# Fused chunked attention and MoE layer on one core: attention values as one 64-column product per head instead of two 32-column products

## The chip, the cores and the metric

The kernel runs on one core of a Trainium2 chip. The metric is the device time of one execution in microseconds (us). Three runs of the kernel before gave 625.8, 627.71 and 628.86 us; the median is 627.71 us.

## What is computed

Two stages, one after the other. First attention in chunks: batch 4, 8 heads, 768 positions, head width 64. Each chunk of 32 queries of a head sees its own 32 keys, 16 to the left, 8 to the right, and 8 memory keys, 64 keys in all. Cut to what matters:

```python
for c in range(nc):                                    # 24 chunks of 32 queries
    k_full = np.concatenate([mem_k, k_ctx], axis=2)    # 8 memory + 56 context rows
    v_full = np.concatenate([mem_v, v_ctx], axis=2)
    scores = scale * np.matmul(q_c, k_full.transpose(0, 1, 3, 2))
    a = softmax(scores)
    out[:, :, c_start:c_end] = np.matmul(a, v_full)    # the values: 32 queries x 64 columns
...
x = attn_out as (3072 tokens, 512)
h = x @ w_in                                           # 512 -> 2048
g = s * relu(h)**2 + b
return g @ w_out                                       # 2048 -> 512
```

## The kernel before, in words

**Tiling.** The 3072 tokens are worked on in 8 chunks of 384 (a "chunk" from here on; the 32-query pieces are called cells). For each chunk there are 16 steps, one per 128 columns of the hidden layer. A step has a first product (`hidden`, line 610: 12 matmuls of 128 loaded columns and 384 moved columns), four ScalarE passes and one VectorE pass (lines 618 to 622), and a second product (`result`, line 633: 9 matmuls of 512 moved columns, two steps later). Operands are split into a high and a low part, which is why there are three matmuls where one product is meant. So one step is 21 matmuls with 21 weight loads on TensorE, 42 instructions.

**Attention** for a later chunk is worked out between the steps of the chunks before it. One call of `attend` takes four heads (two pairs, `p`) of one chunk. From the third chunk on (`alone` is false) it lays one fixed row of TensorE work, called a block here: the values of the attention call before (`value1`, `value2`, one per pair, line 502), then the scores of this call (`scores1`, `scores2`, line 481). Lines 561 to 571 chain these four, so that nothing stands between them. Most blocks are eight steps apart; the first two are six apart. There are 12 value parts in the kernel, the first at 145 us; the last one has no scores behind it.

**The value product** (`value`, lines 490 to 503). The loaded operand is the value tile `vals_[p]`: 128 rows are two cells of 64 keys, and 64 columns are one head's width. The moved operand is the block-diagonal tile `aT`: 64 columns, 32 queries for each of the two cells. Output rows are the 64 columns of the head, head `n` on rows 64n to 64n+63. Before, each head's 64 columns are loaded in two parts of 32, each into a quarter of the array's columns:

```python
for n, e in ((n, e) for n in range(2) for e in range(0, D, CHUNK)) if not alone else ():
    nc.tensor.matmul(V[p].tile[n * D + e:n * D + e + CHUNK, to:to + 2 * CHUNK], vals_[p].tile[:, at(n) + e:at(n) + e + CHUNK],
                     aT[n].tile[:, 2 * p + m, c, :], start=True, stop=True)
```

These operands are plain fp32, and each such matmul is carried out as two pairs of a load and a matmul. So a pair of heads is 2 x 3 x 4 = 24 products, 48 loads and 48 matmuls; both pairs are 96 and 96. The scores of a block are likewise 96 and 96. A block is 384 instructions.

For the first two chunks (`alone`) another form stands in line 498: 64 loaded columns and 32 moved ones, in quarters of 64 rows by 64 columns. The change does not touch it.

**Order.** The order of instructions on every engine is made ahead by a planner (`Plan.lay`). It simulates the engines with a cost for each kind of operation (`HOLD`, line 80, in ns), starts whatever is ready with the lowest due time, and the program is written out in that order. The costs steer the order alone; nothing waits for them on the chip. There are no loops or branches left in the program: every instruction stands in it once.

## Time and profile before

| what | value |
|---|---|
| median of three runs | 627.71 us |
| the profiled execution's own time | 625.31 us |
| its span, first to last instruction | 623.5 us |
| granted TensorE clock, mean | 0.996 |
| TensorE matmul (PE) busy | 97% of the span |
| weight load (PEld) busy | 85% |
| VectorE, ScalarE busy | 55%, 55% |
| chain that ended last | PE 82%, DVE 11%, DMA 4%, issue 2%, ACT 1% |

How to read it. Times are microseconds unless marked ns. PE is TensorE's matmul, PEld its weight load, which runs beside the matmuls. "128*32" behind an instruction is the part of the array that it uses, rows by columns; "128x64" is the moved operand of a matmul, or the loaded operand of a load. A row of the timeline gives the start, the length up to the end of the last instruction in it, the instruction, how many of them follow one another, and in brackets the idle time before it and what ended it. "issue" is time in which the engine waited for nothing that the profile shows. Ends of matmuls are modelled, so distances between starts are the safer measure. A row of stretches gives the stretch, its length, and for each engine the busy time and the number of instructions.

### The profile page before, as it was taken

What the parts mean: (1) busy time and instruction counts of PE and PEld (TensorE: products, weight loads), DVE (VectorE), ACT (ScalarE), POOL (GpSimd) and SP (SyncE); (2) the same over time, 40 slices, a digit from 0 to 9 for tenths busy, and PEclk for the clock granted to TensorE, in tenths of its full rate; (3) what the DMA queues carried; (4) which work ended last, traced back from release to release, by engine and by line L of the source; (5) the groups of instructions that cost most, each with busy time, mean ns of one, the idle gap of its engine ahead of it and who ended that gap; (6) DMA issues with size and microseconds to landing.
All of it is one profiled execution on the core that took longest, in us unless ns stands there. A gap on an engine that the chain in (4) does not pass through costs nothing.

```text
span 623.5 us, 13759 instructions
## 1 busy us (share of the span) xinstructions
PE 605.3 (97%) x5854; PEld 532.3 (85%) x5861; DVE 341.3 (55%) x816; ACT 343.7 (55%) x660; POOL 37.2 (6%) x46
## 2 busy tenths in 40 slices
PE   8898999999999999999999999999999999999997
PEld 5667888888989898898988899898988989899996
DVE  6899999884565462825538182654618355131112
ACT  3577888854555554454455555545555445545543
POOL 2112000000010000101001010100101000000000
PEclk9899999999999999999999999999999999999999
DMA  9944766413041300303022030312103110010001
GB/s 348 400 159 145 243 188 183 131 50 129 1 128 50 112 18 12 134 34 128 1 82 98 2 128 1 129 50 77 53 2 127 52 53 0 2 50 2 1 0 52
DMA packets 17342, 55.42 MB, mean 89 GB/s; under 512 B 1920, under 2 KB 1920, under 8 KB 17280
## 3 DMA queue, kind: packets, MB, share of 16 engines
q1 hardware_dynamic: 17280, 54.53, 25.4%
q8 instruction: 46, 0.75, 0.5%
q14 instruction: 16, 0.13, 0.1%
HBM read 48.24 MB, written 6.29 MB: 87 GB/s over the span
## 4 chain that ended last, share of the span: by engine, by line
PE 82%; DVE 11%; DMA 4%; issue 2%; ACT 1%; POOL 0%; DVEq 0%; SPq 0%; ACTq 0%
PE ps L610 37%; PE ps L633 37%; DMA words<-w 4%; PE ps L502 3%; PE ps L481 3%; DVE wv L591 2%; DVE wv L593 2%; PE ps L371 1%; DVE top L419 1%; DVE t L420 1%; DVE den L422 1%; DVE gL L622 1%; DVE w L597 1%; DVE ww L597 1%; DVE words L589 1%
## 5 line engine op out<-in xcount | busy, mean ns | idle before, releaser
L622 DVE TENSOR_TENSOR gL<-ps,gH 128x384 fp32r<-128x384 f32 x128 | 70.9, 555 | 232.1 <-ACT gH L621 231.2
L618 ACT ACTIVATE ps<-ps 128x384 f32<-128x384 f32 x128 | 60.8, 475 | 191.5 <-PE ps L610 190.5
L610 PE MATMUL ps<-xH,w 128*128 128x384 f32 x512 | 130.9, 336 | 0.3 <-DVE w L597 0.3
L610 PE MATMUL ps<-xH,ww 128*128 128x384 f32 x512 | 130.7, 336 | 0.0
L633 PE MATMUL ps<-w,gH 128*128 128x512 f32 x384 | 119.1, 391 | 0.0
L633 PE MATMUL ps<-ww,gH 128*128 128x512 f32 x384 | 119.0, 391 | 0.0
L610 PEld LDWEIGHTS ps<-xH,w 128*128 128x128 f32 x512 | 92.7, 188 | 3.0 <-DVE w L597 0.9
L610 PEld LDWEIGHTS ps<-xH,ww 128*128 128x128 f32 x512 | 92.8, 188 | 2.2
L440 DVE STREAM_TRANSPOSE aT<-t 32x128 f32<-32x128 f32 x288 | 86.9, 302 | 7.2 <-POOL t L425 2.7
L610 PE MATMUL ps<-xL,w 128*128 128x384 f32 x256 | 87.4, 341 | 2.0 <-DVE top L419 1.3
L610 PE MATMUL ps<-xL,ww 128*128 128x384 f32 x256 | 86.8, 339 | 0.0
L620 ACT ACTIVATE ps<-ps,b_sb,s_sb 128x384 f32<-128x384 f32 x128 | 82.3, 643 | 4.2
L633 PEld LDWEIGHTS ps<-ww,gH 128*128 128x128 f32 x384 | 72.1, 188 | 13.3
L633 PEld LDWEIGHTS ps<-w,gH 128*128 128x128 f32 x384 | 72.1, 188 | 13.2
L633 PE MATMUL ps<-w,gL 128*128 128x512 f32 x192 | 76.3, 398 | 1.2 <-DVE gL L622 1.0
L633 PE MATMUL ps<-ww,gL 128*128 128x512 f32 x192 | 75.9, 395 | 1.1 <-DVE gL L622 1.1
L621 ACT ACTIVATE gH<-ps 128x384 fp32r<-128x384 f32 x128 | 62.9, 491 | 3.9
L619 ACT ACTIVATE ps<-ps 128x384 f32<-128x384 f32 x128 | 60.8, 475 | 4.0
L425 POOL TENSOR_TENSOR t<-t,rden 96x512 f32<-96x512 f32 (+1 forms) x36 | 34.8, 967 | 471.2 <-DVE rden L424 372.9
L610 PEld LDWEIGHTS ps<-xL,w 128*128 128x128 f32 x256 | 48.0, 187 | 5.4 <-DVE top L419 1.4
L610 PEld LDWEIGHTS ps<-xL,ww 128*128 128x128 f32 x256 | 48.0, 187 | 2.8
L633 PEld LDWEIGHTS ps<-w,gL 128*128 128x128 f32 x192 | 36.0, 187 | 8.7 <-DVE gL L622 2.4
(51 smaller groups left out, 439.9 us busy)
## 6 DMA issues: line engine op xcount, KB each, us to landing
raw<-qkv SPq DMA_DIRECT2D x28, 576.0 KB, 6.0
words<-w SPq DMA_DIRECT2D x24, 512.0 KB, 4.0
v<-qkv SPq DMA_DIRECT2D x28, 384.0 KB, 3.9
out<-partial SPq DMA_DIRECT2D x24, 256.0 KB, 2.1
early<-w SPq DMA_DIRECT2D x8, 512.0 KB, 10.5
early<-qkv SPq DMA_DIRECT2D x3, 576.0 KB, 6.4
early<-qkv SPq DMA_DIRECT2D x4, 384.0 KB, 8.5
early<-qkv SPq DMA_DIRECT2D x1, 577.0 KB, 3.7
```

What stands on the lines that cost most here:

```text
L425: op("POOL", "norm" + size, late + 0.25, lambda: nc.gpsimd.tensor_tensor(tv(), tv(), wide(rden), ALU.mult), (st["r", key],), (t[key],), lo ...
L440: nc.vector.transpose(aT.tile[rows, :, c, r * CHUNK:(r + 1) * CHUNK], t.tile[c * CHUNK:(c + 1) * CHUNK, r::2, g * CHUNK:(g + 1) * CHUNK])
L481: nc.tensor.matmul(S[n].tile[c * CHUNK:(c + 1) * CHUNK, (at * GB + j) * CELL:(at * GB + j + 1) * CELL], raw.tile[rows, k * CHUNK:(k + 1) * ...
L502: nc.tensor.matmul(V[p].tile[n * D + e:n * D + e + CHUNK, to:to + 2 * CHUNK], vals_[p].tile[:, at(n) + e:at(n) + e + CHUNK], aT[n].tile[:, ...
L591: op("DVE", "wjoin", due, lambda: nc.vector.scalar_tensor_tensor(bits(), bits(), 3, lo(), ALU.logical_shift_left, ALU.bitwise_or), (raw["l ...
L610: nc.tensor.matmul(h.tile[:, :TOK], weight_tile(0, f)[:, wi, c * P:(c + 1) * P], xt(x, xi, c), start=(c == 0 and n == 0), stop=(c == NC_T ...
L618: op("ACT", "relu", u, lambda: nc.scalar.activation(hp(), hp(), AF.Relu), (), (h[0],))
L619: op("ACT", "square", u, lambda: nc.scalar.activation(hp(), hp(), AF.Square), (), (h[0],))
L620: op("ACT", "affine", u, lambda: nc.scalar.activation(hp(), hp(), AF.Identity, scale=s_sb, bias=b_sb), (c_s[0], c_b[0]), (h[0],))
L621: op("ACT", "high", u, lambda: nc.scalar.activation(g.tile[0], hp(), AF.Copy), (h[0],), (g["H"],))
L622: op("DVE", "low", u, lambda: nc.vector.tensor_tensor(g.tile[1], hp(), g.tile[0].bitcast(F32), ALU.subtract), (h[0], g["H"]), (g["L"],))
L633: nc.tensor.matmul(acc.tile, g.tile[gi][:, t * P:(t + 1) * P], weight_tile(1, f)[:, wi, :], start=(first and n == 0), stop=(last and n == 2))
```

## The change

The cost of `value1` and `value2` in the planner's table goes from 670 to 730 ns, and the value product from the third chunk on takes a head's 64 columns at once:

```diff
-HOLD = dict(hidden=523, result=690, scores=560, value1=670, value2=670, scores1=540, scores2=540, turn=84, value=1300, wrest=1000, warm=215,
+HOLD = dict(hidden=523, result=690, scores=560, value1=730, value2=730, scores1=540, scores2=540, turn=84, value=1300, wrest=1000, warm=215,
...
-                    for n, e in ((n, e) for n in range(2) for e in range(0, D, CHUNK)) if not alone else ():
+                    for n in range(2) if not alone else ():
                         to = (m * NQC + c) * 2 * CHUNK
-                        nc.tensor.matmul(V[p].tile[n * D + e:n * D + e + CHUNK, to:to + 2 * CHUNK], vals_[p].tile[:, at(n) + e:at(n) + e + CHUNK],
+                        nc.tensor.matmul(V[p].tile[n * D:(n + 1) * D, to:to + 2 * CHUNK], vals_[p].tile[:, at(n):at(n) + D],
                                          aT[n].tile[:, 2 * p + m, c, :], start=True, stop=True)
```

The same numbers are multiplied and the same output rows are written. A product uses half of the array's columns instead of a quarter, and there are half as many products: 12 for a pair of heads instead of 24.

## Rows read from the trace of the kernel before

**Rows 1.** The page, busy time, share of the span and instructions of each engine.
```profile
PE 605.3 (97%) x5854; PEld 532.3 (85%) x5861; DVE 341.3 (55%) x816; ACT 343.7 (55%) x660; POOL 37.2 (6%) x46
```

**Rows 2.** Waits of PE, 145 to 620 us: total us, times, longest us.
```profile
PE ps L481 <- issue: 4.5, 4, 1.2
PE ps L610 <- DVE top L419: 1.3, 1, 1.3
```

**Rows 3.** Timeline of PE, the block at 284 us.
```profile
284.11 1.55 PE L502 MATMUL ps<-aT,v 128*32 128x64 f32 x96
285.59 1.04 PE L481 MATMUL ps<-raw 64*32 64x64 f32 x80
287.84 0.41 PE L481 MATMUL ps<-raw 64*32 64x64 f32 x16 [1.21 <-issue]
288.18 0.45 PE L610 MATMUL ps<-xL,w 128*128 128x384 f32 x1
```

**Rows 4.** Timeline of PE, the block at 358 us.
```profile
357.98 1.55 PE L502 MATMUL ps<-aT,v 128*32 128x64 f32 x96
...
360.61 0.44 PE L610 MATMUL ps<-xL,w 128*128 128x384 f32 x1
```

**Rows 5.** Timeline of PE, four more blocks: 145, 247, 466 and 504 us.
```profile
145.30 1.55 PE L502 MATMUL ps<-aT,v 128*32 128x64 f32 x96
146.78 0.95 PE L481 MATMUL ps<-raw 64*32 64x64 f32 x70
...
149.29 0.44 PE L610 MATMUL ps<-xL,ww 128*128 128x384 f32 x1
...
246.65 1.55 PE L502 MATMUL ps<-aT,v 128*32 128x64 f32 x96
...
250.62 0.45 PE L610 MATMUL ps<-xL,ww 128*128 128x384 f32 x1
...
466.21 1.55 PE L502 MATMUL ps<-aT,v 128*32 128x64 f32 x96
...
470.08 0.44 PE L610 MATMUL ps<-xL,ww 128*128 128x384 f32 x1
...
503.53 1.55 PE L502 MATMUL ps<-aT,v 128*32 128x64 f32 x96
...
507.49 0.44 PE L610 MATMUL ps<-xL,w 128*128 128x384 f32 x1 [1.28 <-DVE top L419]
```

**Rows 6.** Stretches from the end of one long gap to the end of the next.
```profile
148.80:250.00 101.20, 100.09 (x1024) 90.34 (x1024) 53.55 (x139) 52.25 (x100) 6.24 (x6) 1.00 0.20 67
250.00:287.82 37.82, 36.59 (x384) 32.96 (x384) 19.42 (x49) 18.81 (x36) 2.08 (x2) 1.00 0.22 75
287.82:469.70 181.88, 180.82 (x1792) 163.05 (x1792) 91.71 (x236) 94.05 (x180) 10.41 (x10) 1.00 0.18 64
469.70:507.48 37.78, 36.50 (x384) 32.82 (x384) 20.56 (x52) 18.81 (x36) 2.08 (x2) 1.00 0.23 80
```

**Rows 7.** DMA queues, instruction kind: whole run; 285.4 to 286.5 us; 428.7 to 429.9 us.
```profile
q8 instruction: 46, 0.75, 0.5%
...
q8 instruction: 1, 0.02, 5.2%
...
q8 instruction: 1, 0.02, 4.9%
```

**Rows 8.** Stretches from the end of a long gap to the start of a block.
```profile
148.80:430.12 281.32, 278.96 (x2672) 251.51 (x2672) 145.36 (x375) 145.09 (x278) 16.65 (x16) 1.00 0.20 67
...
469.70:503.52 33.82, 33.81 (x192) 30.40 (x192) 17.74 (x46) 17.59 (x34) 2.08 (x2) 1.00 0.20 71
```

**Rows 9.** Loads of 32 and 64 columns (busy us, mean ns, idle), and PE's timeline at 45 us.
```profile
L502 PEld LDWEIGHTS ps<-aT,v 128*32 128x32 f32 x1152 | 16.6, 110 | 4.1 <-issue 4.1
...
L498 PEld LDWEIGHTS ps<-aT,v 64*64 64x64 f32 x192 | 3.0, 135 | 0.6 <-issue 0.6
...
45.00 1.60 PE L498 MATMUL ps<-aT,v 64*64 64x32 f32 x96
```

## The prediction

> **What bounds the kernel now.** The page first: TensorE's matmuls fill 97% of the span, VectorE and ScalarE 55% each [rows 1]. So time can come only from TensorE: from the length of its work or from its idle time. The list of waits then says where it is idle behind 145 us, where the changed code runs: four times in the scores, with nothing that the profile can name as the cause ("issue"), and once at the first matmul of a step, 5.8 us in all [rows 2]. No wait for another engine is left in the value parts. The last one is put down to a VectorE instruction which that matmul does not read from; I take it for one of the same kind, for a reason that follows.

> The timeline shows what such a gap is. A clean block runs from 357.98 to 360.61, 2.63 us [rows 4]. The block at 284 us stops 80 matmuls into its scores and takes 4.07 us [rows 3]. The four others with a gap take 3.99, 3.97, 3.87 and 3.96 us [rows 5]. Over the clean length they lose 1.44 + 1.36 + 1.34 + 1.24 + 1.33 = **6.7 us**. The other six blocks with scores have no gap; the one at 358 us stands for them.

> Why in five blocks and not in all? Count where the border of a piece falls. At 504 us, 384 instructions lie between the end of a gap and the block's start [rows 8], so a border is 128 instructions into the block and the next at 384, its end: a gap. At 284 us the gap comes after 192 + 160 = 352 instructions [rows 3], so the border before it is at 96. At 145 us it comes after 332 [rows 5]: 76. The same count gives 48 and 80 for the blocks at 247 and 466 us. At 430 us, 5344 instructions after a border [rows 8], borders fall at 32 and 288, and there is no gap: the fetch packet is already seen at 428.7 to 429.9 us, before the block, since TensorE reads ahead over the slow steps. In the block at 284 us the border at 96 is passed at about 284.11 + 96 x 1.48/192 = 284.85, the packet lies within 285.4 to 286.5 [rows 7], and work goes on at 287.84. So the next piece is usable 3.0 us after its border is passed (the same sum gives 2.9 at 145 and 3.0 at 504 us). A block burns 256 instructions in under 2 us. A gap needs **two borders in one block**, the first of them not read ahead: 48 to 128 here.

> **The change, part by part.**

> *Half the instructions.* A value part goes from 96 loads and 96 matmuls to 48 and 48; a block from 384 instructions to 288. Two borders fit inside only when the first is within the first 32 instructions, and up to there they were read ahead (the block at 430 us). A period of eight steps is 8 x 42 + 384 = 720 instructions before and 624 after. So the first borders of the twelve value parts, before at 76, 208, 0, 48, 96, 144, 192, 240, 32, 80, 128, 152, will be at 76, 48, 192, 80, 224, 112, 0, 144, 32, 176, 64, 184. The tightest is 48: passed about 0.75 us into the block, the next border 16 instructions behind the block's end. A step's instruction takes 33.82/384 = 0.088 us [rows 8], so it is reached 2.7 + 1.4 = 4.1 us into the block, 3.3 us after the first; 3.0 are needed. A small margin, and a miss would cost some tenths. I take all five gaps as gone: **-6.7 us**. Nothing else holds these places: the clean blocks show no wait for another engine behind them, so what is late next is again TensorE's own work.

> *The value product's own pace.* Per pair of heads and pass, a group of four quarter-array products becomes a group of two half-array ones; there are 24 groups in a part before and after, and each still moves 64 columns. What is new is that 64 columns are loaded in the time of such a move. The trace has no load of 64 columns beside 64 moved ones. Nearest is line 498: 64 loaded, 32 moved, also 24 groups, 1.60 us [rows 9] against 1.55 [rows 3], so +0.05 us a part, +0.6 us for 12. The planner's own cost in the diff says 60 ns more for each of 24 products, 1.44 us; its old 670 ns fits what the trace shows (two are 1.34 of the 1.48 us from the value part's start to the scores' [rows 3]). Between 0.6 and 1.4 I take **+1.0 us**. Downward: if instructions alone set the pace, half of them at the scores' 1.15/192 = 6.0 ns would save 0.9 us a part, 11 us in all. I leave it out: the value part now takes 7.7 ns an instruction, more than the scores do on the same engine, so issue is not its limit, and the 24 moves stay. Upward: loads not covered by moves. 32 more columns cost a load 135 - 110 = 25 ns [rows 9], so one of 64 is some 50 ns; wholly in the open that is 50 ns x 24 x 12 = 14.4 us, and if only the added 25 ns shows, 7.2 us.

> *The planner's new cost.* It moves the planned end of a block by 0.12 us and so may swap instructions behind 145 us; before the first value part nothing moves. I price it at nothing: what covers it is VectorE's and ScalarE's 45% of idle time and the absence of waits on them in [rows 2]. If a swap made TensorE wait, one wait would be of the size of the 1.3 us there.

> *What stays.* The change of array form at each end of the value part, the semaphores, the loads of `raw` and `v`, the reads of the result by ScalarE. The value tiles come free within 0.1 us of before, and no queue is passed.

> **Sum.** -6.7 + 1.0 = -5.7 us. Against the profiled execution's 625.31 us that is 619.6 us. That execution lies 2.4 us under the median of the three runs shown; on the median, 627.71 - 5.7 = **622.0 us**.

> **The rivals.** About 0.5%, 3.1 us, is what a measurement of this kernel can tell from no change.

> *Loads in the open (other side).* Two half-array products leave less to run beside a load than four quarter ones. The place is the group of [rows 3], the price 0 to 50 ns a group, 288 groups. At 23 ns it eats the 6.7 us, at 34 ns the kernel is slower by over 0.5%; wholly in the open it is 627.71 - 6.7 + 14.4 = 635.4 us. For it: no such group is in the trace. Against it: loads are busy 85% and matmuls 97% of the same span [rows 1], and line 498's longer loads cost it only 2 ns a group. With only the added 25 ns showing it is 628.2, no change. I give 0.08 to slower and 0.06 to this middle. [...]

> *The gaps are not fetches, or stay.* If the count by 256 is a coincidence or TensorE's next piece is late for another reason, the 6.7 us stay and the pace adds 1.0: 628.7 us, no change. For it: the profile names no cause. Against it: four counts that are all exact multiples of 256. Chance 0.05. [...]

> *Gaps move.* The border rule is read from eleven blocks; if the reading ahead starts a little later than I think, blocks with borders at 32, 48 or 64 keep one. Two gaps of 1.3 us left make it 624.6; chance 0.07, half of it within 0.5%. A swap by the planner that costs two such waits comes to the same; 0.03 more.

> **How the numbers follow.** My case, 622.0 us, has 0.71. Faster by over 0.5%: 0.71 + 0.05 (moved gaps or swaps) = 0.76. Within 0.5%: 0.06 + 0.05 + 0.05 = 0.16. Slower: 0.08. The range starts at 619.0, the lowest run before (625.8) less 6.7 and rounded down, with no pace lost, and ends at 625.5, which takes in two gaps that stay, and a pace 12 ns a group worse than I take it; beyond it lie 0.2.

> **What would show it.** No gap over 0.5 us in any of the eleven blocks, each about 2.7 us from first value matmul to first matmul of a step; 576 value matmuls and 576 loads in place of 1152 each; about 41 instruction packets in place of 46 (1152 fewer instructions are 4.5 pieces); the value part at 1.50 to 1.60 us from its start to the scores'. The prediction is wrong if a gap of over 1 us stands in a block with one border only, or if the value part takes over 2 us.

## The result, and the profile after

The changed kernel takes 619.39 us (median of 4 runs, 618.72 to 619.74), the kernel before 627.89 us (4 runs, 625.8 to 628.86). The ratio is 0.9865, 95% interval 0.9846 to 0.9884: 8.5 us faster, where 5.7 us were forecast. The profiled execution took 619.60 us, with a span of 617.8 us.

The page of the kernel after, the same line as [rows 1]:

```profile
PE 605.0 (98%) x5278; PEld 533.3 (86%) x5285; DVE 341.2 (55%) x816; ACT 344.1 (56%) x660; POOL 37.2 (6%) x46
```

There are 576 matmuls and 576 loads fewer, and TensorE's busy time is the same to 0.3 us: what went is idle time. The view of waits that gave [rows 2] lists nothing at all for PE now between 140 and 612 us. The order of the work on all engines is the one of before, instruction by instruction but for the value products; so the planner's new cost moved nothing.

The timeline of two blocks of the kernel after, the fifth (which had a gap before, [rows 3]) and the seventh (which had none, [rows 4]):

```profile
281.92 1.62 PE L502 MATMUL ps<-aT,v 128*64 128x64 f32 x48
283.47 1.22 PE L481 MATMUL ps<-raw 64*32 64x64 f32 x96
284.62 0.45 PE L610 MATMUL ps<-xL,w 128*128 128x384 f32 x1
...
354.48 1.62 PE L502 MATMUL ps<-aT,v 128*64 128x64 f32 x48
...
357.18 0.45 PE L610 MATMUL ps<-xL,w 128*128 128x384 f32 x1
```

Both take 2.70 us from the first value matmul to the first matmul of the step. Before, they took 4.07 and 2.63. The scores run through without a stop (96 in one row). The value part is 283.47 - 281.92 = 1.55 us long instead of 1.48. All eleven blocks with scores are alike to 0.03 us.

The loads by form, to be read beside [rows 9], and the instruction queue, beside [rows 7]:

```profile
L502 PEld LDWEIGHTS ps<-aT,v 128*64 128x64 f32 x576 | 17.8, 138 | 4.1 <-issue 4.1
```

```profile
q8 instruction: 41, 0.67, 0.5%
```

A load of 64 columns is 28 ns longer than one of 32 (138 against 110), there are half as many, and TensorE's program came in 41 packets instead of 46.

### The profile page after: what moved, and what is told of

Read it like the earlier page. It is cut to its first block, busy times and chain, and to the rows that moved or that the text cites. A ratio compares the mean times of both kernels' runs of the same rounds, so it can differ in the third digit from the quotient of the medians.

```text
span 617.8 us, 12607 instructions
## 1 busy us (share of the span) xinstructions
PE 605.0 (98%) x5278; PEld 533.3 (86%) x5285; DVE 341.2 (55%) x816; ACT 344.1 (56%) x660; POOL 37.2 (6%) x46
## 4 chain that ended last, share of the span: by engine, by line
PE 82%; DVE 11%; DMA 3%; ACT 2%; issue 1%; POOL 0%; DVEq 0%; SPq 0%; ACTq 0%
PE ps L610 37%; PE ps L633 37%; DMA words<-w 3%; PE ps L502 3%; PE ps L481 2%; DVE wv L591 2%; DVE wv L593 2%; PE ps L371 1%; DVE t L420 1%; DVE top L419 1%; DVE ww L597 1%; DVE gL L622 1%; DVE den L422 1%; DVE w L597 1%; DVE words L589 1%
```

## The experiments

Two questions were open: whether the gaps really stand where borders between pieces of 256 instructions fall, and why the gain was 8.5 us and not 5.7. Every kernel was compared with the kernel before on the same chip.

### The program shifted by 112 and by 64 instructions

The kernel before, with small matmuls into an unused bank ahead of everything (56 of them, or 32); nothing else differs.

```diff
     with tc.manual_schedule():
+        for _ in range(56):
+            nc.tensor.matmul(idle[:, :64], ones[:, :P], ones[:, :64], start=True, stop=True)
         for _, _, fn in laid:
             fn()
```

> The kernel before with 56 small matmuls (112 instructions) put ahead of everything, so that every border of a piece falls 112 instructions earlier in the program's own work. Theory: first borders in the eleven blocks move from 76, 208, 0, 48, 96, 144, 192, 240, 32, 80, 128 to 220, 96, 144, 192, 240, 32, 80, 128, 176, 224, 16; so there are three gaps, in the 2nd, 7th and 8th block (near 174, 358 and 394 us), none of the five places of before, and about 2.7 us less idle time behind 145 us. The added matmuls may cost 0 to 3 us at the start. Rival (gaps belong to these places of the work, or to the data): the same five blocks have them.

> The same with 32 small matmuls (64 instructions). Theory: first borders at 12, 144, 192, 240, 32, 80, 128, 176, 224, 16, 64; three gaps, in the 6th, 7th and 11th block (near 322, 358 and 504 us); the one in the 11th block was there before, 2.7 us less idle time behind 145 us. Rival: the same five blocks as before.

Ratios 0.9972 (0.9954 to 0.9990) and 0.9982 (0.9971 to 0.9994). PE's timeline of the kernel shifted by 112, the 2nd, 7th and 8th block, and the 4th, which had a gap before:

```profile
174.13 1.55 PE L502 MATMUL ps<-aT,v 128*32 128x64 f32 x96
175.60 1.04 PE L481 MATMUL ps<-raw 64*32 64x64 f32 x80
177.92 0.41 PE L481 MATMUL ps<-raw 64*32 64x64 f32 x16 [1.27 <-issue]
...
356.39 1.55 PE L502 MATMUL ps<-aT,v 128*32 128x64 f32 x96
357.87 0.97 PE L481 MATMUL ps<-raw 64*32 64x64 f32 x72
359.85 0.45 PE L481 MATMUL ps<-raw 64*32 64x64 f32 x24 [1.01 <-issue]
...
393.66 1.55 PE L502 MATMUL ps<-aT,v 128*32 128x64 f32 x96
395.14 1.22 PE L481 MATMUL ps<-raw 64*32 64x64 f32 x96
397.90 0.45 PE L610 MATMUL ps<-xL,ww 128*128 128x384 f32 x1 [1.54 <-DVE top L419]
...
247.75 1.55 PE L502 MATMUL ps<-aT,v 128*32 128x64 f32 x96
249.23 1.22 PE L481 MATMUL ps<-raw 64*32 64x64 f32 x96
250.38 0.44 PE L610 MATMUL ps<-xL,ww 128*128 128x384 f32 x1
```

Three gaps, in the three blocks named, none of them a block that had one before, and the five old places run clean: 250.38 - 247.75 = 2.63 us. Even the place inside the block is the counted one: a border at 96 puts the next at 352, after 192 value and 160 score instructions, which is the 80 matmuls of the first block here. The gap of the third sits exactly at the block's end, and the profile again puts it down to the VectorE instruction of line 419. That this "wait" moved from the 11th block to the 8th by a shift of the program shows that it never was one.

Shifted by 64, the same view:

```profile
319.66 1.55 PE L502 MATMUL ps<-aT,v 128*32 128x64 f32 x96
321.14 0.97 PE L481 MATMUL ps<-raw 64*32 64x64 f32 x72
323.45 0.45 PE L481 MATMUL ps<-raw 64*32 64x64 f32 x24 [1.34 <-issue]
...
357.61 1.55 PE L502 MATMUL ps<-aT,v 128*32 128x64 f32 x96
...
361.75 0.44 PE L610 MATMUL ps<-xL,w 128*128 128x384 f32 x1 [1.45 <-DVE top L419]
...
503.39 1.55 PE L502 MATMUL ps<-aT,v 128*32 128x64 f32 x96
504.87 0.88 PE L481 MATMUL ps<-raw 64*32 64x64 f32 x64
507.43 0.54 PE L481 MATMUL ps<-raw 64*32 64x64 f32 x32 [1.67 <-issue]
```

Again the three blocks named and no other. The rival, that the gaps belong to certain places of the work, is out; with it goes a collision with the DMA traffic of a place, since the loads of the work stayed where they were in it. PE's waits behind 145 us add up to 3.8 and 4.4 us instead of the 5.8 of [rows 2]: 2.0 and 1.4 us less, where 2.7 were expected, because the gaps that are left are longer on average (1.3 and 1.5 us against 1.2). Besides, the added matmuls let the first value part begin later, at 146.35 and 147.21 us; in the four profiles of the kernel before it begins between 145.30 and 146.04.

### Scores apart from values

The kernel before with its products unchanged; the scores follow a step after the values instead of right behind them.

```diff
-            chain += [op("PE", f"scores{p + 1}", a - 0.05, ...) for p in pairs]
+            chain += [op("PE", f"scores{p + 1}", a + 0.95, ...) for p in pairs]
...
-                o.next = nxt
+                o.next = nxt if o is not chain[1] or not last else None
```

> The kernel before with its products unchanged, but the scores no longer chained to the values: they come a step later, so 192 instructions stand together in place of 384. Theory: no block holds two borders of pieces, so no gap of over 0.5 us in values or scores; 6.7 us less idle time, less about 0.25 us for each of eleven blocks in which the array's form changes twice more, 2.7 us: about 4 us faster than before, ratio 0.993. Rival (the gaps come with the scores' own operands or with the array's form): five gaps or so stay, and the kernel is 2 to 3 us slower than before.

Ratio 0.9906 (0.9892 to 0.9920), 5.9 us faster, where about 4 were expected; PE's waits list nothing between 145 and 610 us. The timeline at the fifth block:

```profile
283.06 1.55 PE L502 MATMUL ps<-aT,v 128*32 128x64 f32 x96
284.54 0.44 PE L610 MATMUL ps<-xL,w 128*128 128x384 f32 x1
...
288.89 1.22 PE L481 MATMUL ps<-raw 64*32 64x64 f32 x96
290.05 0.44 PE L610 MATMUL ps<-xL,w 128*128 128x384 f32 x1
```

The gaps go without a single product being changed. So the change's gain is not that half-array products are better: it is that fewer instructions stand close together. This way round gains less than the change does. From its first value part (146.23 us) to the end of the span it takes 473.7 us; a kernel before free of gaps would take 471.5 by the table further down (30.4 + 441.1). The difference is 2.2 us, 0.2 for each of the eleven blocks in which the array's form changes twice more; the 0.25 of the expectation was the author's estimate. That these changes are its cause fits, but no run took them apart from the changed order of the work. The expectation was too low because the gaps were worth more than 6.7 us, as the last experiment shows.

### Half of the change

The second pair of heads takes products of 64 columns, the first keeps those of 32.

```diff
-                    for n, e in ((n, e) for n in range(2) for e in range(0, D, CHUNK)) if not alone else ():
+                    width = D if p else CHUNK
+                    for n, e in ((n, e) for n in range(2) for e in range(0, D, width)) if not alone else ():
...
-                        nc.tensor.matmul(V[p].tile[n * D + e:n * D + e + CHUNK, to:to + 2 * CHUNK], vals_[p].tile[:, at(n) + e:at(n) + e + CHUNK],
+                        nc.tensor.matmul(V[p].tile[n * D + e:n * D + e + width, to:to + 2 * CHUNK], vals_[p].tile[:, at(n) + e:at(n) + e + width],
```

> Half of the change: the first pair of heads keeps the quarter products of 32 columns, the second takes the half products of 64. A block has 336 instructions, a period of eight steps 672. Theory (a gap where the second border comes less than some 3 us behind the first, which was not read ahead): first borders at 76, 0, 96, 192, 32, 128, 224, 64, 160, 0, 96; so full gaps of 1.2 to 2 us in the 1st and the 8th block (near 145 and 393 us), at most small ones of up to 0.5 us just behind the 3rd and 11th, none elsewhere; value parts of 1.51 us; some 5 us faster than before. Rival (the gain goes with the products' form and not with the count): the same five blocks have gaps, half as long.

Ratio 0.9913 (0.9899 to 0.9927). PE's timeline of the 1st and the 8th block, and of a clean one (the added line shifts the numbers by one):

```profile
145.98 1.73 PE L503 MATMUL ps<-aT,v 128*32 128x64 f32 x72
147.63 1.21 PE L481 MATMUL ps<-raw 64*32 64x64 f32 x94
149.33 0.30 PE L481 MATMUL ps<-raw 64*32 64x64 f32 x2 [0.49 <-issue]
...
392.46 1.73 PE L503 MATMUL ps<-aT,v 128*32 128x64 f32 x72
394.12 1.14 PE L481 MATMUL ps<-raw 64*32 64x64 f32 x88
395.84 0.32 PE L481 MATMUL ps<-raw 64*32 64x64 f32 x8 [0.58 <-issue]
...
283.39 1.73 PE L503 MATMUL ps<-aT,v 128*32 128x64 f32 x72
285.05 1.22 PE L481 MATMUL ps<-raw 64*32 64x64 f32 x96
286.20 0.44 PE L611 MATMUL ps<-xL,w 128*128 128x384 f32 x1
```

The places are the forecast ones, the 1st and the 8th block and no others, so the rival with gaps in the five old blocks is out. Two sizes were missed. A value part is 285.05 - 283.39 = 1.66 us, not 1.51: a change of form in its middle costs some 0.15 us. And the gaps are 0.5 and 0.6 us of idle time instead of 1.2 to 2. That size did not follow from the theory. These blocks are longer, and by the timeline TensorE reaches the second border 2.3 us after it passed the first, so a piece usable 3.0 us after the first leaves 0.7 us idle. Here the pieces were usable after 2.8 and 2.9 us.

### What sets the pace of a half product

The kernel after, with half of each product's moved columns; the values of the second cell of each group are left out.

```diff
-                        nc.tensor.matmul(V[p].tile[n * D:(n + 1) * D, to:to + 2 * CHUNK], vals_[p].tile[:, at(n):at(n) + D],
-                                         aT[n].tile[:, 2 * p + m, c, :], start=True, stop=True)
+                        nc.tensor.matmul(V[p].tile[n * D:(n + 1) * D, to:to + CHUNK], vals_[p].tile[:, at(n):at(n) + D],
+                                         aT[n].tile[:, 2 * p + m, c, :CHUNK], start=True, stop=True)
```

> The kernel after, but each half product moves 32 of its 64 columns (the values of the second cell of each group are left out). If the load of 64 columns sets the pace of a group, a value part stays at 1.53 to 1.55 us from its start to the scores'. If the 64 moved columns set it, the part falls to about 0.8 us. If loads and moves take turns, it falls by half of the moves' share, to about 1.2 us.

The same view as above:

```profile
282.40 1.59 PE L502 MATMUL ps<-aT,v 128*64 128x32 f32 x48
283.92 1.22 PE L481 MATMUL ps<-raw 64*32 64x64 f32 x96
```

The part takes 1.52 us with half of the moves and 1.55 with all. So the moved columns do not set the pace, nor do loads and moves take turns. Of the three cases named the load of 64 columns is left as what sets it; no run changed the load alone.

### The worst places for the kernel after

The kernel after with 20 small matmuls ahead of everything, put in as above.

> The kernel after with 20 small matmuls (40 instructions) ahead of everything: first borders at 36, 8, 152, 40, 184, 72, 216, 104, 248, 136, 24 in the eleven blocks, the worst places for it. Theory: the second border comes 4 instructions behind the 1st block and 8 behind the 4th, 2.5 to 2.8 us after the first, so there are gaps of 0.3 to 1.5 us right behind the 1st and the 4th block if their first border was not read ahead, and none if it was; none in the other nine. At most 2 us slower than the kernel after. Rival (the change removes the gaps wherever the borders fall): no gap at all.

PE's timeline of the 1st and the 4th block:

```profile
147.75 1.62 PE L502 MATMUL ps<-aT,v 128*64 128x64 f32 x48
149.29 1.22 PE L481 MATMUL ps<-raw 64*32 64x64 f32 x96
150.44 0.44 PE L610 MATMUL ps<-xL,ww 128*128 128x384 f32 x1
...
247.80 1.62 PE L502 MATMUL ps<-aT,v 128*64 128x64 f32 x48
249.35 1.22 PE L481 MATMUL ps<-raw 64*32 64x64 f32 x96
250.50 0.44 PE L610 MATMUL ps<-xL,ww 128*128 128x384 f32 x1
```

No gap. Both blocks take the 2.70 us of the others, and PE's waits list nothing between 145 and 610 us. By itself that fits the theory (the first borders, at 36 and 40, were read ahead) as well as the rival. The DMA view tells which, instruction kind, 147.3 to 147.6 us and 247.3 to 247.7 us:

```profile
q8 instruction: 1, 0.02, 20.0%
...
q8 instruction: 1, 0.02, 20.7%
```

A fetch packet is seen before either block starts, as it was for the clean block at 430 us before. In the kernel after as it is, the second block has its border at 48, and its packet comes only 1.2 us into the block (at 174.62 us). So a border up to 40 instructions into a block was read ahead here and one at 48 was not, and blocks of 288 instructions were clean at the borders tried in two layouts of the program. The ratio to before is 0.9879 (0.9861 to 0.9896).

### The spread of the kernel before

The kernel before three more times, and the kernel after once more, unchanged.

> The kernel before once more, unchanged, for its spread. Theory (gaps are late pieces of 256 instructions): the same five gaps of 1.2 to 1.5 us, in the blocks near 145, 247, 284, 466 and 504 us, since the count of instructions is the same; a span within 1 us of 623.5. If executions of the kernel before differ by more than 1 us, the gaps differ in length or number between them, or the first 145 us do. Rival (gaps come from collisions with DMA traffic): gaps at other blocks in this execution.

> The kernel before, a third profile. Theory (the gain on the medians is larger than forecast since the profiled execution of before had short gaps): the gaps stand in the same blocks, their sum differs between executions, between 6.5 and 9.5 us, and the span differs with it, by about the same amount. Rival (the sum of the gaps is 6.7 us whenever it runs, and the rest of the gain comes from elsewhere): 6.5 to 7 us of gaps, with a span above 625 us all the same.

> The kernel before, a fourth profile; the same two expectations as for the third.

> The kernel after once more: no gap of over 0.5 us behind 145 us in its profile; 618.5 to 620 us, ratio to before 0.985 to 0.989; its executions differ less among themselves than those of before, since the length of a gap is what varies there.

The first copy of before gave 0.9996 (0.9978 to 1.0014) of it, and the kernel after 0.9886 (0.9860 to 0.9911), 620.20 us against 628.01. In all four profiles of before the five blocks have their gaps, but the lengths differ; in the first copy the expectations of 1.2 to 1.5 us a gap and of a span within 1 us of 623.5 failed (1.1 to 1.8 us, and 625.0). That the blocks are always the same ones speaks against collisions with DMA traffic once more. PE's timeline of the fifth block in the first copy, to be read beside [rows 3], and of the steps behind its sixth block:

```profile
284.29 1.55 PE L502 MATMUL ps<-aT,v 128*32 128x64 f32 x96
285.77 1.04 PE L481 MATMUL ps<-raw 64*32 64x64 f32 x80
288.60 0.41 PE L481 MATMUL ps<-raw 64*32 64x64 f32 x16 [1.79 <-issue]
288.95 0.44 PE L610 MATMUL ps<-xL,w 128*128 128x384 f32 x1
...
326.33 0.34 PE L610 MATMUL ps<-xH,ww 128*128 128x384 f32 x1
327.12 0.45 PE L610 MATMUL ps<-xH,ww 128*128 128x384 f32 x1 [0.46 <-issue]
```

This block takes 4.66 us instead of 4.07. And a sixth, short gap stands behind a block whose second border falls just after its end; by the counts that border is at 400, 16 instructions behind the block. The second copy has it too (0.44 us), the third has not. The next table adds up each profile: when the first value part starts, what the twelve value parts with their scores take, and what is left.

| profile | first value part | value parts and scores | the rest | span |
|---|---|---|---|---|
| before, on which the forecast rests | 145.3 | 37.1 | 441.1 | 623.5 |
| before, first copy | 145.3 | 38.3 | 441.4 | 625.0 |
| before, second copy | 146.0 | 38.5 | 441.4 | 625.9 |
| before, third copy | 145.9 | 38.4 | 441.1 | 625.4 |
| after | 145.6 | 31.2 | 441.0 | 617.8 |
| after, again | 144.8 | 31.2 | 440.8 | 616.8 |

Free of gaps, the column of value parts and scores would be 11 x 2.63 + 1.48 = 30.4 for before. So the gaps cost 6.7 us in the first profile, and 7.9, 8.1 and 8.0 in the others, with 0.3 more in the rest of two of them. All else behind the first value part stays within 0.4 us. So the expectation for the two later copies holds (gaps in the same blocks, 6.5 to 9.5 us in all), and its rival, gaps of 6.7 us whenever the kernel runs, does not. One more expectation failed: the executions of the kernel after are no closer to one another (618.54 to 624.51), so the length of the gaps is not the only thing that varies; what else does is open.

## Why the prediction was right, and where it was off

**The gaps.** Right in kind, place and cause: all five went, the count by 256 is shown by the two shifted programs, and [rows 2]'s one wait on VectorE was of the same kind. The size was the term that was mis-sized. The step "over the clean length they lose 6.7 us" took its durations from one execution, whose gaps were shorter than in the three others profiled (7.9 to 8.1 us). The prediction saw that this execution lay 2.4 us under the median, and still took its 6.7 us off the median; 1.3 us of the 2.4 are longer gaps. With 8.0 and the measured pace the sum is -7.2 us, against 8.5 measured in the first comparison and 7.8 in the second. What is left of the two is of the size of the differences in when the first value part starts (144.8 to 146.0 us in the six profiles of the table); that it comes from there is not shown. That the time fell into the range owes something to luck: its low end lies only 0.4 us under the measured time, and the reason given for that end, a pace that loses nothing, did not come true.

**The pace.** +1.0 forecast, +0.07 us a part measured, 0.8 us for twelve; the row of line 498 gave 0.6, the planner's cost 1.4. The reason was right in part. Fewer instructions brought the products themselves nothing, as it said. But "the 24 moves stay" was not what holds the pace: half of the moved columns took only 0.03 us off the part, and the load is what is left. Loads in the open, the rival on the other side, fell with the 1.55 us. Had loads and moves taken turns, half of the moves would by the author's estimate have brought the part to about 1.2 us, and it took 1.52.

**The planner's cost.** Priced at nothing, and nothing it was: no order changed.

**The reading ahead.** "3.0 us after its border is passed" was too fixed; over all profiles the pieces were usable 2.8 to 3.7 us after it. In the first copy the fifth block passes its border at about 284.29 + 96 x 1.48/192 = 285.03 and goes on at 288.60, 3.6 us later. The margin of 0.3 us forecast for the tightest border of the kernel after would have been too small for such a piece. Its working also misread a row: the 33.82 us over 384 instructions [rows 8] hold 48 quick score instructions, so one of a step takes some 0.1 us and not 0.088. In the trace the second border is reached 4.19 us into the block, 3.4 us after the first. No gap came there, in two profiles of the kernel after. That executions of it may have one now and then cannot be excluded. And "two borders in one block" was a little too narrow a condition: the sixth gap's second border lies 16 instructions behind its block.

**The rival that the gaps are no fetches** fell with the shifts. Most crossings of a border show no gap at all: there are some 45 per run (46 packets [rows 7]), and behind 145 us five to six of them are seen. Those in the five blocks cost 1.2 to 2.0 us each, the sixth some 0.3; they are the ones at which 256 instructions, nearly all of 6 to 8 ns (1.15/192 us in the scores, 1.48/192 in the values), follow a border that was not read ahead.

No version tried clearly beats the changed kernel. Scores apart, half of the change, and the shifts all lie between the two.

## What to carry to other kernels

Where idle time in dense stretches of small matmuls has no releaser, count instructions from one gap to the next. Here the counts were multiples of 256 [rows 6] and pointed to a program that itself came too late, and a wait of 1.28 us put down to an unrelated instruction [rows 5] was the same thing. Instructions per microsecond were then a cost of their own: one large product instead of two small ones brought 8.5 us, though it made a value part 0.07 us slower, and spreading the small ones out between long ones brought 5.9 us. The gaps of one and the same kernel added up to 6.7 us in one execution and to 8.1 in another; before sizing what the removal of a gap brings, profile the kernel more than once.

## What the runs showed of the hardware that was not expected

In one profile the granted TensorE clock fell after a long gap. In the program shifted by 64, the 11th block stands still before 507.43 us (1.67 us of idle time). The granted clock is 1.00 up to 507 us, 0.84 on the mean of the next 3 us and 0.50 from 510 to 512; if it went from 1.00 to 0.50 in one step, that was some 1.6 us after the gap. Stretches of that profile (the third number from the end is the granted clock):

```profile
505.00:507.00 2.00, 0.75 (x64) 0.59 (x59) 0.97 (x2) 0.49 (x1) 0.00 (x0) 1.00 0.68 195
507.00:510.00 3.00, 2.57 (x41) 2.48 (x42) 1.83 (x5) 0.40 (x1) 0.00 (x0) 0.84 0.47 138
510.00:512.00 2.00, 2.00 (x7) 1.80 (x7) 1.90 (x5) 1.00 (x3) 0.00 (x0) 0.50 0.00 0
```

The rest of that profile, outside the value parts and scores, is 443.0 us instead of 441.1. That these 1.9 us are the price of the lower clock is the author's estimate. Other gaps of this length, up to the 1.79 us above, were followed by no fall that was seen (the mean granted clock is 0.997 in that profile and 0.992 in this one), so what made the difference stays open. A second thing: in the half of the change a value part with a switch from quarter to half products in its middle took 1.66 us, 0.15 more than the 1.51 between the two forms' 1.48 and 1.55. That is twice what the wider product itself costs a whole part, 0.07 us.
